# New order tables for all engines and the transfers, up to the first MLP units of a fused adaLN, linear-attention and MLP block

## The chip, the cores and the metric

The kernel runs on one core of a Trainium2 chip. A core has TensorE (PE in the profile, with its weight loads as PEld), VectorE (DVE), ScalarE (ACT), GpSimd (POOL) and a queue of transfers that SyncE issues (SP). The metric is the device time of one execution in microseconds; the median of three runs of the kernel before is 1084.8.

## What is computed

The reference, cut to what matters (S = 2048 tokens, D = 576, F = 4608, H = 32 heads of 18):

```python
mod = (silu(c) @ w_mod).reshape(1, 6, 1, D)
sa, ca, ga, sb, cb, gb = (mod[:, k] for k in range(6))
h = layernorm(x) * (1 + ca) + sa
q, k, v = heads(h @ wqkv)
pq, pk = phi(q), phi(k)             # phi(t) = where(t > 0, t + 1, exp(t)) + 1e-6
kv = einsum("bhsd,bhse->bhde", pk, v);  z = pk.sum(2)
o = einsum("bhqd,bhde->bhqe", pq, kv) / (einsum("bhqd,bhd->bhq", pq, z) + 1e-6)
x = x + ga * (o @ wo)
h = layernorm(x) * (1 + cb) + sb
x = x + gb * (silu(h @ w1) @ w2)
```

All in and out is float32.

## The kernel before

The program is one function without loops at run time: Python loops write out about 19,000 instructions. It has three parts.

*Stage A* (lines 500 to 1336): the mod columns come from w_mod by sums on VectorE (`add_rows`, L516 and L518, into a tile named hT), which TensorE turns into columns (L527) and, for the last chunk, into rows (`mod_rows`, L538, tile psG) and back into columns (L549); `keep_busy` (L567) puts products of ones between, whose results nobody reads. x is transposed (L556, L1250), its layer norm applied (L351 to L365), and K products for the first block of tokens are `k_part` (L573, tile psK, 56 products of 288 columns). Later blocks' K and Q products are L928. phi goes over ACT and DVE, and splits its result in a high and a low half (L958, L960, tile w); TensorE adds xs transposed times these into psG (L1053), block after block, and DVE adds psG to the sums (L1063, tiles sum_107 to sum_111). kv comes from there (L1186), then the product of kv with wo (L1223). The second set of mod rows runs beside all this through GpSimd and a reduction on DVE (L1110, `crow<-raw`).

*Attention out* (200 to 360 us): per block of 512 tokens the transposes L1357, the products L389, the residual, layer norm, and transposes of h into an hT of its own (L374). For pairs of blocks DVE and GpSimd form the sums of a Strassen-like scheme (`sums`, L1684 to L1687: H and S tiles), ACT and DVE split them into two float16 halves (L1631 and L261 among others), and `store_h` (L1508) sends these combinations, named hd, to device memory. Beside this the first slice of the MLP runs as plain products: up L1432, SiLU and split L1434 and L264 to L267 (tile hs), down L1443 in a PSUM tile `big`, and its addition to the token's accumulator on DVE (`down_add`, L1448, tile acc).

*MLP units* (from about 357 us to the end): Strassen-like up products (L1924) and down products (L2008), with VectorE sums (L1946 to L1948 and L2017 to L2021). The combinations hd are fetched back from device memory into three rooms in turn (`fetch`, L1627, tiles hT, xn, first, w), the raw weights of a unit come by `load1` (L1587 and L1589: 512 KB and two of 64 KB) and `load2` (L1596), and the scan of later weights for their scale by L719.

What sets the order: each engine runs its instructions strictly in the order in which they stand in its stream, and SP issues its transfers in the order in which they stand in its own; an instruction whose operand isn't there holds up all that stand behind it. Stage A is first placed by tables named STAGE_A, the units by a list scheduler. Then `arrange(ORDERS, begun)` (L2379) takes the instructions of each engine in the order in which the program traced them and chains them, by dependencies without a wait, in the order of a table of index ranges, ORDERS. Indices that the table doesn't name follow in the traced order:

```python
def arrange(orders, start):
    for engine, text in orders.items():
        traced = [i for i in nc.cur_bb.bb.instructions[start:]
                  if i.engine == getattr(mybir.EngineType, engine) and listed(i)]
        order = [j for part in text.split() for j in span(part)]
        order += sorted(set(range(len(traced))) - set(order))
        for a, b in zip(order, order[1:]):
            follow(traced[b], traced[a])
```

The table names the first 2991 instructions of TensorE, 656 of VectorE, 489 of ScalarE, 262 of GpSimd and 203 of SP. Waits for operands come from the tiles and are set apart from this.

Of the kernel before, what the change touches and what calls it, by code (L numbers as in the profile page):

```python
# [24 lines left out]
def kernel(ctx: ExitStack, tc, A_x, A_wqkv, A_wo, B_x, B_w1, B_w2, c, w_mod, out):  # L25
# [33 lines left out]
    def behind(instructions):  # L59

        with ExitStack() as order:
# [7 lines left out]
            0-43 45-46 52 49-50 44 47-48 53-54 51 65 57-58 61-62 66-72 55-56 59-60 63-64 73-77 82-83 80-81 78-79  # L69
            84-87 90-91 88-89 92-101 116-118 102-103 124 104-105 119-123 125 106-115 126-141 154-167 142-153  # L70
            168-181 246-251 210-213 182-199 214-215 290-293 216-219 294-295 200-209 220-221 256-267 274-277
            222-223 278-289 224-237 302-307 238-245 252-255 308-311 268-273 330-335 296-301 336-357 312-319
            358-359 320-325 360-367 326-329 368-375 378-383 376-377 386-389 384-385 398-403 390-393 404-405
            394-397 412-423 436-451 406-411 424-435 452-477 490-499 478-489 524-527 500-513 520-523 530-539
            514-519 586-587 528-529 588-589 540-545 554-571 576-579 592-597 590-591 598-599 610-621 600-609
            546-551 646-647 580-581 622-627 582-585 552-553 572-575 648-657 670-671 628-641 672-675 682-683
            642-645 684-687 714-721 658-663 722-723 664-665 692-693 666-669 688-689 694-713 724-725 676-679
            726-727 690-691 728-729 680-681 742-745 730-741 746-791 826-831 792-795 862-863 796-797 864-867
            832-833 872-873 798-813 838-839 814-815 840-853 816-821 854-855 822-823 856-859 874-877 860-861
            868-871 878-889 834-837 890-895 824-825 896-917 926-935 918-921 936-939 922-923 940-947 924-925  # L80
            978-983 1000-1003 950-955 966-975 1004-1005 976-977 984-993 948-949 994-999 1006-1019 1022-1023
            1020-1021 956-965 1024-1035 1050-1055 1036-1049 1056-1063 1084-1085 1064-1077 1102-1105 1086-1087
            1106-1113 1078-1079 1114-1117 1088-1091 1118-1123 1130-1131 1080-1081 1132-1135 1124-1129 1136-1137
            1082-1083 1138-1155 1096-1099 1092-1095 1160-1169 1156-1157 1170-1171 1100-1101 1172-1183 1158-1159
            1184-1219 1236-1237 1248-1259 1220-1221 1285-1286 1222-1227 1238-1247 1228-1235 1287-1296 1260-1262
            1297-1300 1263-1284 1301-1325 1352-1356 1326-1349 1357-1364 1385-1388 1365-1370 1389-1390 1350-1351
            1371-1384 1413-1416 1391-1400 1417-1427 1401-1406 1428-1429 1407-1412 1430-1443 1446-1449 1444-1445
            1451-1468 1450 1479-1486 1469-1478 1507-1511 1487-1506 1512-1535 1540-1544 1536-1539 1545-1568
            1573-1574 1569-1572 1575-1592 1601-1604 1593-1594 1605-1621 1595-1596 1634 1638 1597-1600 1622-1633
            1646-1649 1635-1636 1650 1639-1641 1655-1660 1687-1696 1637 1661-1676 1642-1645 1677-1682 1715-1719  # L90
            1697-1700 1651-1654 1701-1704 1683 1705-1706 1720-1723 1684-1686 1707-1714 1724-1751 1762-1767
            1776-1779 1781-1782 1768-1769 1780 1752-1753 1783-1794 1754-1761 1795-1798 1770-1772 1799-1800
            1773-1775 1801-1810 1821-1825 1854 1870-1873 1855-1857 1826-1835 1811-1820 1836-1843 1874 1858
            1875-1877 1844-1853 1859-1860 1883 1915 1884-1886 1861-1863 1916-1918 1878-1881 1887-1888 1882
            1864-1869 1889-1914 1919-1921 1931-1935 1976 1922-1927 1936-1939 1928-1930 1990-1993 1940-1941 1994
            1977-1978 1995-1996 1942-1971 2004-2007 1972-1975 1979-1982 2008-2010 1983-1984 2011-2012 1985-1988
            2013-2018 1989 2019-2036 1997-2003 2037 2049-2061 2082-2083 2098-2101 2062-2069 2086-2088 2070-2077
            2038-2045 2084-2085 2046-2048 2078-2081 2089 2102-2103 2090-2093 2106-2110 2094 2111-2112 2104
            2113-2114 2095-2097 2115-2122 2105 2123-2140 2143 2141-2142 2147 2159-2166 2144-2145 2167-2172 2146
            2173-2178 2187 2179-2186 2188 2199-2202 2189-2190 2203 2191 2204-2210 2213-2214 2148-2149 2215-2216  # L100
            2192-2198 2211-2212 2150-2158 2217 2231-2234 2218-2223 2235-2238 2224-2230 2239-2241 2249 2259-2262
            2245 2255-2258 2246-2248 2242 2263-2264 2243-2244 2265-2269 2295 2250 2296-2299 2251-2253 2270
            2309-2313 2254 2283 2271 2284-2285 2277-2278 2286-2293 2300 2294 2301-2302 2314 2303 2279 2304-2308
            2272-2276 2280-2282 2315-2324 2329 2335-2338 2325 2339-2340 2330-2331 2326-2328 2341 2332-2334
            2347-2356 2342-2346 2359-2360 2357 2361-2369 2358 2370-2377 2391 2378-2382 2392-2398 2383 2399-2404
            2384-2390 2405-2422 2427-2431 2423-2424 2433-2438 2432 2445-2450 2425-2426 2463-2470 2439-2444
            2451-2454 2483-2488 2503-2505 2457-2462 2489-2490 2506-2508 2455-2456 2555-2557 2521-2528 2471-2472
            2477 2473 2478 2474 2567 2479-2480 2475 2481-2482 2541-2542 2476 2543-2544 2568-2572 2545-2546 2491
            2547-2548 2558-2560 2492-2495 2497-2500 2496 2501-2502 2579-2584 2509-2520 2585-2586 2529-2537
            2593-2595 2538-2540 2549-2550 2596-2600 2551-2554 2561-2566 2607-2612 2573-2578 2587-2591 2619-2626  # L110
            2592 2633-2640 2601-2606 2647-2652 2613-2615 2627-2629 2616-2618 2630-2632 2659-2661 2641-2646
            2653-2654 2662-2663 2655-2658 2664-2692 2739-2740 2693-2698 2705-2708 2741-2742 2709-2710 2699-2704
            2733-2735 2719-2720 2743 2711-2718 2721-2732 2736-2738 2744-2762 2783-2794 2775-2782 2815-2820
            2795-2798 2873 2799-2800 2874-2875 2801 2763-2764 2802 2765 2876 2766-2767 2877-2878 2768-2774
            2833-2840 2803-2814 2853-2860 2821 2841 2822 2891 2842-2844 2929 2892-2895 2823-2830 2845-2852
            2930-2936 2879-2881 2909-2912 2831-2832 2882-2887 2913-2915 2888-2890 2916 2861-2867 2896-2898
            2868-2872 2899-2908 2949-2953 2917-2919 2954 2920-2921 2937-2939 2922-2928 2967-2974 2940-2943
            2955-2962 2944-2948 2963-2965 2987-2990 2975-2977 2966 2978-2986
        """,
        "DVE": """  # L120
# [2290 lines left out]
```

## Time and profile before

| | |
|---|---|
| three runs | 1084.69, 1084.8, 1085.23 us |
| span of the profiled execution | 1085.1 us |
| TensorE busy | 1063.3 us, 98% of the span |
| weight loads | 760.6 us, 70% |
| VectorE busy | 893.0 us, 82% |
| ScalarE busy | 707.3 us, 65% |
| GpSimd busy | 737.6 us, 68% |
| device memory | 177 GB/s over the span, read 176.77 MB, written 15.48 MB |
| granted TensorE clock | 0.93 in the first 25 us, 1.00 in each later window |

The profile is of one execution, 0.3 us longer than the median of the runs. A line of the timeline gives the start, the time from there to the end of the last of a run of like instructions, the engine, the line of the kernel, the operation with its tiles, and in brackets the engine's idle time before it and what ended that. A row of the waits gives the waiting line, the releaser, the idle time in total, how often, and the longest. Matmuls overlap, so a matmul's own length is longer than the distance from one start to the next.

### The profile page before, as it was taken

The numbers are of one execution on the slowest core, as the hardware profiler recorded it, in microseconds if no ns is written. First come the engines' busy times: TensorE is split into PE (matmuls) and PEld (weight loads), VectorE is DVE, ScalarE is ACT, GpSimd is POOL, SyncE is SP. The second block draws the span as 40 slices with busy tenths as digits, with TensorE's granted clock in tenths as the row PEclk, the third lists the DMA queues.
The fourth block names the chain that finished last, engine by engine and source line by source line (L and its number), as shares of the span: only waits on it lengthen the run. The fifth ranks groups of instructions, "written<-read, shape, count | busy, mean of one in ns | idle before, by whom it ended". The sixth has DMA issues, their size and how long they took to land.

```text
span 1085.1 us, 19052 instructions
## 1 busy us (share of the span) xinstructions
PE 1063.3 (98%) x7027; PEld 760.6 (70%) x7027; DVE 893.0 (82%) x1438; ACT 707.3 (65%) x1318; POOL 737.6 (68%) x804
## 2 busy tenths in 40 slices
PE   8999999999999899999999999999999999999998
PEld 6999999898885455666666666666666666666665
DVE  7966857788889899988987988987987887898767
ACT  4866553248667777777667667767766776676554
POOL 3467524654725589879888778877778678677563
PEclk9999999999999999999999999999999999999999
DMA  8497954224256877387577577567667657626422
GB/s 294 143 178 202 101 148 119 70 83 127 61 165 195 240 250 254 125 250 230 175 223 213 182 217 222 171 223 203 200 196 234 201 154 252 206 68 201 165 80 109
DMA packets 119341, 193.50 MB, mean 178 GB/s; under 512 B 42892, under 2 KB 77584, under 8 KB 119248
## 3 DMA queue, kind: packets, MB, share of 16 engines
q1 hardware_dynamic: 86276, 190.81, 56.6%
q10 hardware_dynamic: 32972, 1.48, 3.1%
q8 instruction: 55, 0.90, 0.4%
q14 instruction: 38, 0.31, 0.1%
HBM read 176.77 MB, written 15.48 MB: 177 GB/s over the span
## 4 chain that ended last, share of the span: by engine, by line
PE 80%; DVE 9%; DMA 4%; ACT 2%; POOL 2%; issue 1%; SPq 0%; DVEq 0%; POOLq 0%; ACTq 0%
PE up L1924 31%; PE down L2008 30%; PE big L389 5%; PE psK L928 4%; PE psG L1053 4%; PE big L1443 2%; DMA raw<-parts 1%; DMA hT<-hd 1%; PE small L1432 1%; DVE hT L261 1%; PE small L374 1%; DMA raw<-in_w_mod_dram 1%; DVE w L261 1%; PE big L1357 1%; PE psK L1223 1%
## 5 line engine op out<-in xcount | busy, mean ns | idle before, releaser
L1924 PE MATMUL up<-hT,w 128*128 128x512 f16 x1264 | 317.9, 379 | 2.2 <-DMA hT<-hd 2.2
L1924 PEld LDWEIGHTS <-w 128*128 128x128 f16 x1492 | 145.8, 98 | 136.1 <-DMA hT<-hd 2.9
L2017 DVE SCALAR_TENSOR_TENSOR acc<-acc,set,down 128x576 f32<-128x576 f32 x128 | 103.6, 810 | 33.8 <-PE down L2008 32.9
L1942 ACT ACTIVATE f<-f,set 128x512 f32<-128x512 f32 x102 | 73.3, 719 | 63.6 <-DVE f L1948 52.1
L1962 POOL TENSOR_TENSOR s<-f,f 128x256 f32<-128x256 f32 x66 | 54.6, 827 | 77.4 <-ACT f L1943 75.3
L2008 PE MATMUL down<-w,hc 128*128 128x288 f16 x600 | 90.6, 286 | 0.1
L2008 PE MATMUL down<-w,hb 128*128 128x288 f16 x600 | 89.3, 286 | 0.6 <-DVE U L2019 0.5
L2008 PE MATMUL down<-w,hT 128*128 128x288 f16 x480 | 82.8, 286 | 0.4 <-DVE acc L2021 0.4
L1946 DVE TENSOR_TENSOR f<-up,p 128x512 f32<-128x512 f32 x102 | 69.6, 682 | 13.8 <-PE up L1924 9.4
L1943 ACT ACTIVATE f<-f,set 128x512 f32<-128x512 f32 x102 | 73.6, 722 | 3.2
L2008 PEld LDWEIGHTS <-hb 128*128 128x128 f16 x600 | 58.7, 98 | 22.7 <-issue 1.4
L2008 PEld LDWEIGHTS <-hc 128*128 128x128 f16 x600 | 58.7, 98 | 22.0 <-issue 0.4
L1986 POOL TENSOR_TENSOR hc<-s,hc 128x512 f16<-128x512 f32 x50 | 63.9, 1278 | 6.0 <-ACT hc L1982 6.0
L1948 DVE TENSOR_TENSOR f<-up,f 128x512 f32<-128x512 f32 x68 | 46.8, 689 | 25.4 <-PE up L1924 24.3
L2008 PEld LDWEIGHTS <-hT 128*128 128x128 f16 x480 | 46.9, 98 | 26.6 <-issue 0.8
L1966 POOL TENSOR_TENSOR f<-f,s 128x256 f32<-128x256 f32 x66 | 53.4, 809 | 17.3 <-DVE hb L1986 10.2
L1959 POOL TENSOR_TENSOR s<-f 128x256 f32<-128x256 f32 x66 | 57.0, 864 | 9.5 <-ACT f L1939 4.5
L1964 POOL TENSOR_TENSOR s<-s,f 128x256 f32<-128x256 f32 x66 | 56.3, 853 | 3.5
L389 PE MATMUL big<-w,qT 128*128 128x288 f32 x352 | 58.6, 304 | 0.0
L2008 PE MATMUL down<-w,hd 128*128 128x288 f16 x396 | 55.5, 286 | 0.2 <-DVE acc L2017 0.2
L2008 PE MATMUL down<-w,ha 128*128 128x288 f16 x396 | 55.7, 286 | 0.0
L1053 PE MATMUL psG<-w,xs 128*128 128x288 f32 x336 | 52.2, 296 | 1.3 <-DVE sum L1063 1.3
(408 smaller groups left out, 2805.3 us busy)
## 6 DMA issues: line engine op xcount, KB each, us to landing
hT<-hd SPq DMA_DIRECT2D x101, 640.0 KB, 4.6
hT<-hd SPq DMA_DIRECT2D x65, 512.0 KB, 3.7
hT<-in_B_w_dram SPq DMA_DIRECT2D x14, 576.0 KB, 6.4
hT<-in_B_w_dram SPq DMA_DIRECT2D x28, 256.0 KB, 5.8
raw<-in_B_w_dram SPq DMA_DIRECT2D x11, 576.0 KB, 6.2
v<-in_B_w_dram SPq DMA_DIRECT2D x9, 576.0 KB, 4.9
acc<-in_A_x_dram SPq DMA_DIRECT2D x16, 288.0 KB, 4.3
raw<-in_B_w_dram SPq DMA_DIRECT2D x9, 512.0 KB, 5.2
```

The source lines that it names most:

```text
L389: T.matmul(ps, xpart(a), wpart(b), start=n == 0, stop=n == len(XW) - 1)
L1053: T.matmul(ps[:, h, :HALF], l, pk[t][:, u, h * HALF : (h + 1) * HALF], start=t == 0 and m == 0, stop=t == 3 and m == len(left) - 1)
L1924: T.matmul(ps, left, right, start=first and m == 0, stop=m == len(seq) - 1, skip_group_check=True)
L1942: A.activation(f, f, AF.Silu, scale=factor(self.g, "inv"))
L1943: A.activation(f, f, AF.Identity, scale=factor(self.g, "delta"))
L1946: V.tensor_add(f, self.bank[bank[1]], self.p1)
L1959: G.tensor_sub(self.s3, half(i, 0, 0), half(i, 0, 1))
L1962: G.tensor_add(self.s[:, 0:1], half(i, 0, 1), half(i, 1, 1))
L1964: G.tensor_sub(self.s[:, 1:2], self.s[:, 0:1], half(i, 0, 0))
L1986: eng.tensor_sub(t[:, :, 1, :], src, t[:, :, 0, :])
L2008: T.matmul(ps[:, p, :HALF], left[:, u, p * P : (p + 1) * P], right[:, v], start=n in (1, 5, 7, 6) and j == 0, stop=j == len(passes) - 1, s ...
L2017: V.scalar_tensor_tensor(dst, dst, factor(self.g, "ratio"), ps[:, :, :HALF], op0=ALU.mult, op1=ALU.add)
```

## The change

The five tables of ORDERS are replaced by others, found offline. No instruction is altered, added or left out, and each new table names the same indices as the old. STAGE_A and all else are the same. The new tables take 13 lines more, so that every line behind them has a number 13 higher in the changed kernel (L1448 becomes L1461, L1627 becomes L1640).

```diff
     ORDERS = {
         "PE": """
-            0-43 45-46 52 49-50 44 47-48 53-54 51 65 57-58 61-62 66-72 55-56 59-60 63-64 73-77 82-83 80-81 78-79
...
+            0-19 22-23 26 31-35 27-28 38 41-42 20-21 24-25 29-30 36-37 51 39-40 65 52 66-70 43 71-72 45-46 49-50 73-77
...
```

The instructions of the two kernels stand in the same order from about 450 us of the profile before on. Ahead of that most of them move, by a few microseconds of the engine's work. Three places:

TensorE at the head of the program: `psK<-w,hT` are the K products, `psG<-hT,ones` and `psG<-tmod,sc` the mod rows, `psG<-ones` the products that only keep TensorE busy, `psG<-ident` the rows turned into columns. Before:

```order
L527 MATMUL psG_116<-ones,hT 128x1 x2
L567 MATMUL psG_117<-ones 128x128
L527 MATMUL psG_116<-ones,hT 128x1 x2
L567 MATMUL psG_117<-ones 128x128 x2
L573 MATMUL psK<-w,hT 128x288 x3
L538 MATMUL psG_116<-tmod,sc 1x320
L573 MATMUL psK<-w,hT 128x288 x7
L538 MATMUL psG_117<-tmod,sc 1x320
L538 MATMUL psG_117<-hT,ones 1x320
L573 MATMUL psK<-w,hT 128x288 x4
L538 MATMUL psG_116<-hT,ones 1x320
```

and now:

```order
L540 MATMUL psG_116<-ones,hT 128x1 x2
L551 MATMUL psG_117<-tmod,sc 1x320
L540 MATMUL psG_116<-ones,hT 128x1 x2
L551 MATMUL psG_117<-hT,ones 1x320
L551 MATMUL psG_116<-tmod,sc 1x320
L551 MATMUL psG_116<-hT,ones 1x320
L580 MATMUL psG_117<-ones 128x128 x4
L586 MATMUL psK<-w,hT 128x288
L562 MATMUL psG_117<-ident,e 128x1
L562 MATMUL psG_117<-ident,zsum 128x1
L586 MATMUL psK<-w,hT 128x288 x4
```

The first K product has moved behind all four row products, ten of the others with it.

VectorE in stage A, at about 130 to 141 us of the profile before: `w<-a,w` is the low half of phi, `sum<-psG,sum` empties a PSUM bank, `crow<-raw` is the long reduction. Before:

```order
L1020 STREAM_TRANSPOSE acc_94<-xt 128x18x32 x4
L494 SCALAR_TENSOR_TENSOR a<-z,a 128x576
L494 SCALAR_TENSOR_TENSOR a<-e,a 128x576
L960 SCALAR_TENSOR_TENSOR w<-a,w 128x576 x2
L1063 TENSOR_TENSOR sum_107<-psG_116,sum_107 128x576
L1110 TENSOR_REDUCE crow<-raw_122 128x9
L1063 TENSOR_TENSOR sum_108<-psG_117,sum_108 128x576
```

and now:

```order
L1033 STREAM_TRANSPOSE acc_94<-xt 128x18x32 x4
L507 SCALAR_TENSOR_TENSOR a<-z,a 128x576
L507 SCALAR_TENSOR_TENSOR a<-e,a 128x576
L1123 TENSOR_REDUCE crow<-raw_122 128x9
L507 SCALAR_TENSOR_TENSOR a<-z,a 128x576
L973 SCALAR_TENSOR_TENSOR w<-a,w 128x576 x2
L1076 TENSOR_TENSOR sum_107<-psG_116,sum_107 128x576
L374 TENSOR_SCALAR acc_93<-acc_93,col_a 128x512 x2
L1076 TENSOR_TENSOR sum_108<-psG_117,sum_108 128x576
```

The reduction has moved from behind w and the first sum to ahead of both. On TensorE the first product that reads w of the token tile xs_114 has 836 matmuls ahead of it now, and 872 before.

VectorE and SP from the last plain MLP products to the first Strassen-like ones, 338 to 374 us. VectorE: `acc` is the addition of a down product, `H` and `S` are the sums of the combinations. Before:

```order
L267 SCALAR_TENSOR_TENSOR hs<-sl,set_99,hs 128x512
L261 TENSOR_TENSOR hT<-sl,hT 64x512
L1684 TENSOR_TENSOR H<-H,S 128x512
L1685 TENSOR_TENSOR S<-S 128x512
L1448 SCALAR_TENSOR_TENSOR acc_93<-acc_93,set_99,big 128x576
```

and now:

```order
L280 SCALAR_TENSOR_TENSOR hs<-sl,set_99,hs 128x512
L274 TENSOR_TENSOR hT<-S,hT 128x512
L1461 SCALAR_TENSOR_TENSOR acc_93<-acc_93,set_99,big 128x576
L274 TENSOR_TENSOR hT<-S,hT 128x512
L274 TENSOR_TENSOR hT<-sl,hT 64x512
L1697 TENSOR_TENSOR H<-H,S 128x512
L1698 TENSOR_TENSOR S<-S 128x512
```

SP, where `hT<-hd` fetches a combination and `raw` and `hT<-in_B_w` are weights. Before:

```order
L1627 DMA hT<-hd_2140 128x2048
L1589 DMA raw<-in_B_w_dram 64x256
L1587 DMA raw<-in_B_w_dram 128x4x256
L719 DMA hT<-in_B_w_dram 64x4x256 x2
L1627 DMA hT<-hd_2141 128x2560
L1627 DMA hT<-hd_2142 128x2560
L1627 DMA hT<-hd_2133 128x2048
```

and now:

```order
L1640 DMA hT<-hd_2140 128x2048
L1602 DMA raw<-in_B_w_dram 64x256
L1521 DMA hd_2142<-hT 128x512
L1640 DMA hT<-hd_2141 128x2560
L1640 DMA hT<-hd_2142 128x2560
L1602 DMA raw<-in_B_w_dram 64x256
L732 DMA hT<-in_B_w_dram 64x4x256
L1640 DMA hT<-hd_2133 128x2048
L1609 DMA raw<-in_B_w_dram 128x2x576
L1640 DMA hT<-hd_2134 128x2048
L1600 DMA raw<-in_B_w_dram 128x4x256
```

The addition to acc has moved ahead of the sums on VectorE, and on SP the fetches of hd_2141 and hd_2142 ahead of the 512 KB of raw weights and of the weights for the scan; a store of a part of hd_2142 stands right in front of them.

229 lines of the change are left out of this document (121 added, 108 removed).

## The prediction

> **What bounds the kernel now.** I read the page's busy shares first, then the busy time by stretches of the program, then the waits of TensorE, and last the timeline at the few places where TensorE waits longest. The change reaches only up to about 450 us, so the question at each step is how much of TensorE's time ahead of 450 us is not work. The first line of the page, and the windows (span of the window, then busy time of PE, PEld, DVE, ACT, POOL with their instructions, granted clock, DMA share, GB/s):
>
> ```profile
> PE 1063.3 (98%) x7027; PEld 760.6 (70%) x7027; DVE 893.0 (82%) x1438; ACT 707.3 (65%) x1318; POOL 737.6 (68%) x804
> ...
> 0.00:36.00 36.00, 30.96 (x186) 25.60 (x187) 27.59 (x66) 19.91 (x38) 11.49 (x15) 0.95 0.78 255
> 36.00:240.00 204.00, 200.06 (x1478) 196.44 (x1477) 147.34 (x252) 106.88 (x166) 113.63 (x87) 1.00 0.59 131
> 240.00:359.00 119.00, 114.06 (x809) 93.00 (x808) 106.69 (x191) 80.99 (x136) 56.31 (x54) 1.00 0.47 146
> 359.00:450.00 91.00, 87.75 (x507) 49.12 (x506) 82.87 (x132) 70.72 (x145) 76.06 (x93) 1.00 0.69 214
> ...
> 325.00:425.00 100.00, 93.97 (x560) 54.59 (x559) 91.49 (x145) 72.79 (x143) 69.30 (x81) 1.00 0.75 231
> 450.00:475.00 25.00, 25.00 (x170) 16.42 (x169) 22.56 (x36) 17.17 (x35) 19.71 (x25) 1.00 0.68 213
> ```
>
> TensorE is the bound: 98% busy, and full in the window from 450 us on. Ahead of 450 us it is idle for 5.04 us up to 36, 3.94 up to 240, 4.94 up to 359 and 3.25 up to 450 (each window less its first number): 17.2 us. That is the ceiling of any gain from order alone, since the tables change no product. And because TensorE is full right behind 450 us, whatever it gains or loses before goes through to the end one for one.
>
> Where the 17.2 us lie is told by TensorE's waits from 240 to 359 us and then the longest from 359 to 450 us (waiting line, releaser, total, times, longest):
>
> ```profile
> PE big L1443 <- DVE acc L1448: 1.9, 1, 1.9
> PE up L1924 <- DVE acc L1448: 0.8, 1, 0.8
> PE big L1443 <- ACT hs L264: 0.7, 1, 0.7
> PE big L1443 <- DVE qT L261: 0.5, 1, 0.5
> PE big L1443 <- DVE hs L267: 0.5, 1, 0.5
> PE big L1357 <- DVE qT L261: 0.3, 1, 0.3
> PE small L374 <- ACT sl L1434: 0.3, 1, 0.3
> ...
> PE up L1924 <- DMA hT<-hd: 2.2, 1, 2.2
> ```
>
> Two waits of about 2 us stand out, the first row of each part. Both are a matter of who stands in front in a queue, which is what the tables set.
>
> **The change part by part.** Nothing is removed or added; instructions only stand elsewhere. A wait that goes is a gain by its length; an instruction that now stands ahead of its operand makes one.
>
> *The accumulator behind the sums (338 to 342 us).* DVE and, last, TensorE around the 1.9 us:
>
> ```profile
> 338.83 1.65 DVE L1684 TENSOR_TENSOR H<-H,S 128x512 f32<-128x512 f32 x1
> 340.58 1.11 DVE L1685 TENSOR_TENSOR S<-S 128x512 f32<-128x512 f32 x1
> 341.61 0.80 DVE L1448 SCALAR_TENSOR_TENSOR acc<-acc,set,big 128x576 f32<-128x576 f32 x1
> ...
> 342.47 1.88 PE L1443 MATMUL big<-w,hs 128*128 128x288 f16 x14 [1.87 <-DVE acc L1448]
> ```
>
> The addition to acc frees the PSUM bank that the next down product writes. It takes 0.80 us, but two strips of Strassen sums (1.65 and 1.11 us) run in front of it. In the new DVE table the first acc addition stands ahead of both, so it can end 2.8 us earlier than 342.41, before TensorE reaches its product at 340.6. The wait is 1.87 us and should go whole: **-1.9**. What comes late instead is the sums, by the 0.80 us of the addition: they are stored as hd and fetched from there for the MLP units, some 20 us later (the next rows), so there is cover.
>
> *The stored combination behind weight loads (361 to 374 us).* SP's issues, TensorE's wait, and the time to landing of the transfers of this stretch (queue, count, KB each, median us):
>
> ```profile
> 361.43 0.47 SPq L1589 DMA_DIRECT2D raw<-in_B_w_dram  x1
> 361.96 0.58 SPq L1587 DMA_DIRECT2D raw<-in_B_w_dram  x1
> 362.63 1.29 SPq L719 DMA_DIRECT2D hT<-in_B_w_dram  x2
> 366.24 9.74 SPq L1627 DMA_DIRECT2D hT<-hd  x4
> ...
> 374.17 1.47 PE L1924 MATMUL up<-hT,w 128*128 128x512 f16 x6 [2.17 <-DMA hT<-hd]
> ...
> hT<-hd SPq DMA_DIRECT2D x4, 640.0 KB, 7.7
> xn<-hd SPq DMA_DIRECT2D x1, 640.0 KB, 4.0
> ...
> hT<-in_B_w_dram SPq DMA_DIRECT2D x3, 256.0 KB, 7.8
> raw<-in_B_w_dram SPq DMA_DIRECT2D x1, 512.0 KB
> raw<-in_B_w_dram SPq DMA_DIRECT2D x1, 64.0 KB, 4.1
> ...
> hT<-hd SPq DMA_DIRECT2D x101, 640.0 KB, 4.6
> ```
>
> The fetch of hd_2141 is issued at 366.24 and releases TensorE at 374.17, 7.9 us later, while a fetch of the same size in the same stretch, with nothing large ahead of it (xn), took 4.0, and over the whole program the median is 4.6 (the last row, of the page). Ahead of the slow one in the queue are 1,088 KB of weights (64, 512 and two of 256 KB). In the new SP table both fetches (2141 and 2142) stand ahead of the 512 KB and of the two of 256 KB. The issue itself can hardly be earlier, since it waits for the up products to leave its room. So it lands at 366.24 + 4.0 to 4.6 = 370.2 to 370.8, before the 372.0 at which TensorE asks for it: **-2.2**. If the transfers behind it share the engines from the start, 7.9 stays, and the term is nothing. The weights land later by the 1,280 KB now ahead, some 4 us; they are split and used units later.
>
> *The other waits from 240 to 359 us.* They are 0.8 + 0.7 + 0.5 + 0.5 + 0.3 + 0.3 = 3.1. Counting the work ahead of each waiting product and of its releaser in both orders, with the durations of this trace, the releasers of the larger ones (hs, the last acc before L1924) stand 1.3 to 3.6 us nearer to the front than their products do. That speaks for all of it, but such counts hold only while the engine that releases is not itself held up. I take half, **-1.5**, with 0 and -3.1 as bounds.
>
> *The head (0 to 36 us).* TensorE's K products (L573) and what they stand among:
>
> ```profile
> 14.69 0.80 PE L573 MATMUL psK<-w,hT 128*128 128x288 f32 x3 [0.59 <-ACT hT L365]
> 16.05 1.21 PE L573 MATMUL psK<-w,hT 128*128 128x288 f32 x7
> 18.78 0.70 PE L538 MATMUL psG<-hT,ones 128*1 128x320 f32 x2 [0.90 <-DVE hT L518]
> 20.93 1.23 PE L538 MATMUL psG<-hT,ones 128*1 128x320 f32 x2
> 33.77 2.47 PE L928 MATMUL psK<-wq,hT 128*128 128x288 f32 x17
> ...
> 15.89 2.84 DVE L518 SCALAR_TENSOR_TENSOR hT<-hT,sc 128x640 f32<-128x640 f32 x2
> ```
>
> Before, 10 of the 56 K products run while DVE still adds up the mod rows, and the K block is done at 33.8. In the new PE order all four row products (L538) stand ahead of the first K product. They need DVE's last L518, which ends at 15.89 + 2.84 = 18.73, so the first K product starts at about 19.5 instead of 14.7, with TensorE almost idle before. From there on the block is tighter: 56 products at 0.13 us each (the row of 17 on L928: 2.47 / 17 = 0.145, less its tail) are 7.3 us, and the small products among them (L567, L549, L1250) some 5, so 31.8 without any wait. With about 1 us of waits, as much as the block of before had behind 24 us, it is 32.8 against 33.8: **-1.0**. Bounds: -2.6 when the block starts early and waits for nothing; +4.8 when the whole block moves by its later start, 19.5 - 14.7.
>
> [...] The granted clock is 0.95 up to 36 us and 1.00 in each later window. [...]
>
> *New waits.* Nothing in the trace has their length, so I bound them by the places where an order comes closest to its operand. The nearest is stage A from 130 to 142 us:
>
> ```profile
> 132.03 1.62 DVE L960 SCALAR_TENSOR_TENSOR w<-a,w 128x576 fp32r<-128x576 f32 x2 [1.25 <-ACT w L958]
> 138.07 0.76 DVE L1063 TENSOR_TENSOR sum<-psG,sum 128x576 f32<-128x576 f32 x1 [4.42 <-PE psG L1053]
> 138.74 2.33 DVE L1110 TENSOR_REDUCE crow<-raw 128x9 f32<-128x1152 f32 x1
> ...
> 136.28 0.95 PE L1053 MATMUL psG<-w,xs 128*128 128x288 f32 x6
> ```
>
> In before the low half w is ready at 133.65 and its first product starts at 136.28, 2.6 us in hand. In the new orders that product stands 36 products nearer to the front (4.7 us at 0.13), and on DVE the reduction of 2.33 us stands ahead of w: up to 4.7 + 2.3 - 2.6 = 4.4 us of wait, from which comes what DVE's 4.42 idle us take up. Bounds for all new waits are 0 and 9 (two or three such places, as below). I take **+2.0**, nearer to nothing, since DVE is busy only 147.34 of 204.00 us from 36 to 240 and can catch up.
>
> **Sum.** -1.9 - 2.2 - 1.5 - 1.0 + 2.0 = -4.6. The profiled span is 1085.1 us and the median of the runs shown 1084.8, 0.3 less; taken off the median, 1084.8 - 4.6 = **1080.2**.
>
> **The rivals.**
> *Slower: stage A starves.* The 4.4 us at w come whole, and the sums L1063, which stand behind the same reduction and w, hold the next PSUM bank for another 2 to 3 us, then once more at the last block of stage A: three waits of 3 us. Gains kept: -6.6; new waits +9.0; sum +2.4, 1087.2. For it: TensorE waits 1.3 us for those sums in this stage already, twice. Against it: DVE is idle over a quarter of this stretch. It decides against the change once the new waits are over 6.6 + 2.2 us.
> *No change: VectorE takes it back.* From 325 to 425 us DVE is busy 91.49 of 100 us. If TensorE comes 4.1 us earlier, DVE must do the same work with half of its 8.5 us of idle time, and its order is bound to PSUM banks that come free one by one. The two large waits then come back as waits for L2017 and L2021 behind 375 us: -1.5 - 1.0 + 2.0 = -0.5, 1084.3. Against it: DVE's 22.56 of 25 us in the window from 450, where TensorE waits for nothing.
> *No change: the head loses.* +4.8 in place of -1.0, the other terms kept: +1.2, 1086.0. For it: TensorE starts K 4.8 us later, and what it did in that time still has to be done. Against it: the small products that kept it from K behind 19 us are then done. The clock: its loss up to 36 us, 0.05 x 36 = 1.8 us, is paid once more on the K block: -4.6 + 1.8 = -2.8, 1082.0.
> *More.* All waits of 240 to 374 us go and none is new: -1.9 - 2.2 - 3.1 - 1.0 = -8.2, 1076.6.
> That the change doesn't do what it says is no rival: the listed order has the moves.
>
> **How the numbers follow.** A measurement of this kernel can tell some 0.2%, 2.2 us, from no change: under 1082.6 is faster, over 1087.0 slower. Forecast 0.45, the clock's case 0.05, more 0.10: faster 0.60. VectorE 0.16 and the head 0.07: same 0.23. Stage A 0.17: slower. The range goes from all terms at their best with no new wait, -1.9 - 2.2 - 3.1 - 2.6 = -9.8, 1075.0, to stage A's 1087.2; the likeliest case alone holds 1077 to 1082.6.
>
> **What would show each step.** Right: no wait of L1443 for acc over 0.5 us near 340, none of L1924 for hd near 370, hd_2141 landing within 5 us of its issue, L928 beginning at or before 33.8, TensorE full from 450 us on but with everything 4 to 5 us earlier. Wrong: waits of psG for sum or w of over 2 us between 128 and 150 us, waits for L2017 or L2021 of over 1 us between 375 and 450, a granted clock under 0.95 up to 36 us, or a stretch before 240 us that ends later than now. The prediction falls if the time is over 1082.6, and its reason falls if the time is under it but both 2-us waits are still there.

## The result, and the profile after

The changed kernel took 1090.57 us in the median of 4 runs (1090.06 to 1093.48), the kernel before 1084.74 beside it (1083.59 to 1085.23). The ratio is 1.0064, with an interval of 1.0048 to 1.0080: slower by about 6 us, where 1080.2 was forecast and 1087.2 was the upper end.

The profiled execution of the changed kernel has a span of 1088.6 us and took 1090.37, so a time is its span and some 1.75 us. By that the profile of before (span 1085.1) is of an execution of about 1086.9, and not of a typical one: 73 further runs of before, in three groups, lie between 1081.5 and 1087.3, with medians of 1083.98, 1083.96 and 1084.09.

First the busy times of the page and the same four windows as before (span, then busy PE, PEld, DVE, ACT, POOL, granted clock, DMA share, GB/s), of the changed kernel:

```profile
PE 1066.5 (98%) x7027; PEld 763.9 (70%) x7027; DVE 872.1 (80%) x1438; ACT 707.4 (65%) x1318; POOL 732.8 (67%) x804
...
0.00:36.00 36.00, 30.74 (x198) 27.19 (x199) 27.32 (x74) 23.15 (x46) 11.12 (x15) 0.95 0.84 270
36.00:240.00 204.00, 198.45 (x1439) 193.90 (x1438) 130.68 (x233) 105.78 (x162) 105.73 (x84) 0.98 0.61 134
240.00:359.00 119.00, 115.36 (x810) 94.56 (x809) 99.30 (x190) 77.50 (x126) 59.78 (x55) 0.99 0.38 120
359.00:450.00 91.00, 87.67 (x511) 49.47 (x509) 82.63 (x136) 68.08 (x139) 72.73 (x89) 1.00 0.76 235
```

TensorE's idle time is now 5.3, 5.6, 3.6 and 3.3 us, 17.8 in all against 17.2: the order gained nothing on balance. And the same 7027 products kept it busy for 1066.5 us instead of 1063.3, with a granted clock of 0.98 and 0.99 where before had 1.00. The 0.6 us of waits and the 3.2 us of slower products are the 3.5 us between the two spans, to a few tenths.

Then TensorE's waits of the changed kernel from 240 to 359 us and, last, from 359 to 450 us (waiting line, releaser, total, times, longest):

```profile
PE small L1445 <- ACT hT L1653: 1.1, 1, 1.1
PE small L1445 <- DVE hT L274: 1.0, 2, 0.7
PE small L387 <- DVE xn L366: 0.7, 1, 0.7
PE big L1370 <- DVE acc L1461: 0.4, 1, 0.4
PE big L1456 <- DVE acc L1461: 0.2, 1, 0.2
...
PE up L1937 <- DMA hT<-hd: 2.9, 2, 2.6
```

The waits that the prediction named are gone: none for acc near 340 us beyond the 0.2 of the fifth row, none for hd near 370 (the 2.6 us of the last row stand at 432). Others have come. Where, is told by comparing when TensorE has done the same amount of work in the two traces. By that lag (plus is later) the changed kernel loses 16.3 us in four short stretches and gains 12.5 elsewhere:

| stretch, us of before | lag gained or lost | lag at its end |
|---|---|---|
| 0 to 90 | -2.4 | -2.4 |
| 90 to 100 | +3.6 | +1.2 |
| 100 to 210 | -2.4 | -1.2 |
| 210 to 230 | +4.8 | +3.7 |
| 230 to 320 | -0.9 | +2.8 |
| 320 to 340 | +4.6 | +7.4 |
| 340 to 420 | -6.0 | +1.4 |
| 420 to 430 | +3.2 | +4.6 |
| 430 to the end | -0.8 | +3.8 |

The 6.0 us from 340 to 420 hold what was forecast for the accumulator and the fetch. The four losses are these.

*The accumulator's load, 210 to 230 us.* The changed kernel's issues of SP, then DVE and TensorE that wait for the last of them (start, length, and in brackets the idle time before):

```profile
209.73 0.34 SPq L815 DMA_DIRECT2D acc<-in_A_x_dram  x1
210.24 1.32 SPq L732 DMA_DIRECT2D w<-in_B_w_dram  x2
211.66 0.56 SPq L1389 DMA_DIRECT2D raw<-in_B_w_dram  x1
212.26 0.50 SPq L800 DMA_DIRECT2D acc<-in_A_x_dram  x1
...
219.31 0.76 DVE L1384 TENSOR_TENSOR acc<-big,acc 128x576 f32<-128x576 f32 x1 [6.54 <-DMA acc<-in_A_x_dram]
...
220.12 1.07 PE L402 MATMUL big<-w,qT 128*128 128x288 f32 x6 [3.05 <-DVE acc L1384]
```

and the same load in the kernel before:

```profile
198.80 4.33 SPq L787 DMA_DIRECT2D acc<-in_A_x_dram  x2
```

The new SP table sets this load of x behind three loads of weights, whose own turn doesn't come before 210 us. It goes out 13.5 us later, behind their bytes, and lands 7.0 us after its issue; DVE stands 6.54 us for it, and TensorE 3.05 for DVE.

*The reduction, 90 to 100 us.* DVE and TensorE of the changed kernel:

```profile
83.06 2.40 DVE L1123 TENSOR_REDUCE crow<-raw 128x9 f32<-128x1152 f32 x1 [2.70 <-DMA raw<-parts]
85.39 2.72 DVE L1033 STREAM_TRANSPOSE acc<-xt 128x576 f32<-128x576 f32 x4
...
89.62 0.53 PE L1066 MATMUL psG<-w,xs 128*128 128x288 f32 x2 [0.70 <-ACT w L971]
90.97 0.53 PE L1066 MATMUL psG<-w,xs 128*128 128x288 f32 x2 [0.83 <-DVE w L973]
```

DVE's reduction stands in front of its transposes and of the steps that make w, and waits 2.70 us for its own transfer. All behind it is late, and TensorE waits 0.70 us for w's high half and 0.83 for its low one.

*The cast, 320 to 340 us.* ACT and TensorE of the changed kernel:

```profile
329.03 1.62 ACT L364 ACTIVATE xn<-acc,mv 128x576 f32<-128x576 f32 x2 [4.15 <-PE small L387]
330.56 0.60 ACT L1653 CAST hT<-H 128x512 f16<-128x512 f32 x1
...
331.21 0.59 PE L1445 MATMUL small<-hT,w 128*128 128x512 f16 x2 [1.11 <-ACT hT L1653]
```

ACT's cast hT stands behind a layer norm that waits 4.15 us for TensorE, and TensorE waits 1.11 us for the cast. Of the rows of waits above, 0.38 of the second, the 0.71 of the third (DVE's layer norm behind the residual addition) and the 0.17 of the fifth lie in this stretch too: 2.4 us in all. The other 0.66 of the second row stands at 270 us.

*The store, 420 to 430 us.* SP and TensorE of the changed kernel:

```profile
425.08 0.42 SPq L746 DMA_DIRECT2D limits<-raw  x1
427.17 0.32 SPq L1640 DMA_DIRECT2D hT<-hd  x1
...
434.55 0.38 PE L1937 MATMUL up<-hT,w 128*128 128x512 f16 x1 [2.55 <-DMA hT<-hd]
```

The fetch of hd_2142 now stands behind a store of limits, is issued at 427.17 and releases TensorE 7.4 us later. The wait before it, 0.32 us for a fetch, lies in this stretch too.

The losses are larger than the waits in them: 3.6 for 1.5 (0.70 + 0.83), 4.8 for 3.05, 4.6 for 2.4, 3.2 for 2.9 (2.55 + 0.32). The trace records TensorE's granted clock, and behind three of the four waits it falls to one half. Windows of the changed kernel, two by two, the one with the wait and the next:

```profile
88.00:91.40 3.40, 1.88 (x12) 1.41 (x12) 2.56 (x4) 2.61 (x4) 1.41 (x1) 1.00 0.75 216
91.48:94.89 3.41, 3.41 (x17) 3.41 (x16) 1.39 (x2) 0.97 (x2) 3.16 (x2) 0.50 0.76 201
217.80:221.10 3.30, 0.98 (x7) 0.98 (x8) 1.79 (x3) 2.77 (x4) 0.00 (x0) 1.00 0.41 102
221.19:224.60 3.41, 3.41 (x17) 3.41 (x16) 2.38 (x6) 0.00 (x0) 2.26 (x2) 0.50 0.44 127
330.40:333.80 3.40, 1.50 (x8) 0.76 (x8) 2.89 (x8) 2.38 (x5) 1.99 (x3) 1.00 0.97 325
333.83:337.24 3.41, 3.41 (x13) 1.71 (x14) 1.66 (x2) 1.46 (x2) 3.41 (x4) 0.50 0.38 100
```

What such a window costs is read from the distance between products. The first two rows lie in the second window of half clock, the others behind it:

```profile
221.37 1.65 PE L402 MATMUL big<-wq,hT 128*128 128x288 f32 x6
222.81 1.17 PE L402 MATMUL big<-w,qT 128*128 128x288 f32 x4
...
225.47 0.70 PE L402 MATMUL big<-w,qT 128*128 128x288 f32 x4
226.00 0.42 PE L402 MATMUL big<-v,qT 128*128 128x288 f32 x2
```

Six products take 222.81 - 221.37 = 1.44 us, 0.24 each; behind the window four take 0.53, 0.13 each. So a window full of these float32 products costs 3.41 x (1 - 0.13 / 0.24) = 1.5 us; float16 ones of 512 columns stand 0.43 us apart in the window from 333.83 (three from 333.93 to 335.23) and 0.22 behind it (three from 338.43 to 339.08), which makes 1.7. Then 1.5 + 1.5 = 3.0 stand for 3.6 measured, 3.05 + 1.5 = 4.6 for 4.8, 2.4 + 1.7 = 4.1 for 4.6, and without a window 2.9 for 3.2. The four places are thereby accounted for, to 0.6 us each. Each of the three windows of half clock is 3.41 us long in the trace, and in the 3.3 to 3.4 us ahead of each TensorE worked for 0.98 to 1.88 us.

### The profile page after: what moved, and what is told of

It reads as the page before. It is cut to its first block, busy times and chain, and to the rows that moved or that the text cites. A ratio compares the mean times of both kernels' runs of the same rounds, so it can differ in the third digit from the quotient of the medians.

```text
span 1088.6 us, 19038 instructions
## 1 busy us (share of the span) xinstructions
PE 1066.5 (98%) x7027; PEld 763.9 (70%) x7027; DVE 872.1 (80%) x1438; ACT 707.4 (65%) x1318; POOL 732.8 (67%) x804
## 4 chain that ended last, share of the span: by engine, by line
PE 77%; DVE 5%; DMA 4%; ACT 1%; issue 1%; SPq 0%; POOL 0%; DVEq 0%; ACTq 0%; POOLq 0%
PE up L1937 32%; PE down L2021 30%; PE big L402 5%; PE psK L941 2%; PE psG L1066 2%; PE small L1445 1%; DMA hT<-hd 1%; PE big L1456 1%; DVE hT L274 1%; DMA acc<-in_A_x_dram 1%; DMA acc<-turned 1%; PE big L1370 1%; PE small L387 1%; PE down L2055 1%; PE up L2055 1%
## 5 line engine op out<-in xcount | busy, mean ns | idle before, releaser
L1937 PE MATMUL up<-hT,w 128*128 128x512 f16 x1264 | 322.0, 379 | 2.9 <-DMA hT<-hd 2.9
L2021 PE MATMUL down<-w,hc 128*128 128x288 f16 x600 | 91.4, 286 | 0.0
L2021 PE MATMUL down<-w,hb 128*128 128x288 f16 x600 | 91.3, 286 | 0.1
L2021 PE MATMUL down<-w,hT 128*128 128x288 f16 x480 | 82.8, 286 | 0.4 <-DVE acc L2034 0.4
L2021 PEld LDWEIGHTS <-hb 128*128 128x128 f16 x600 | 58.7, 98 | 25.9 <-issue 3.2
L2021 PEld LDWEIGHTS <-hc 128*128 128x128 f16 x600 | 58.6, 98 | 22.6 <-POOL hc L1999 0.2
L402 PE MATMUL big<-w,qT 128*128 128x288 f32 x352 | 62.7, 311 | 3.0 <-DVE acc L1384 3.0
L2021 PEld LDWEIGHTS <-hT 128*128 128x128 f16 x480 | 46.9, 98 | 26.6 <-issue 0.8
L1066 PE MATMUL psG<-w,xs 128*128 128x288 f32 x336 | 55.6, 296 | 1.5 <-DVE w L973 0.8
L2021 PE MATMUL down<-w,ha 128*128 128x288 f16 x396 | 56.5, 286 | 0.1
L2021 PE MATMUL down<-w,hd 128*128 128x288 f16 x396 | 56.3, 286 | 0.0
```

Of the source, the lines that this page charges most:

```text
L402: T.matmul(ps, xpart(a), wpart(b), start=n == 0, stop=n == len(XW) - 1)
L1066: T.matmul(ps[:, h, :HALF], l, pk[t][:, u, h * HALF : (h + 1) * HALF], start=t == 0 and m == 0, stop=t == 3 and m == len(left) - 1)
L1937: T.matmul(ps, left, right, start=first and m == 0, stop=m == len(seq) - 1, skip_group_check=True)
L2021: T.matmul(ps[:, p, :HALF], left[:, u, p * P : (p + 1) * P], right[:, v], start=n in (1, 5, 7, 6) and j == 0, stop=j == len(passes) - 1, s ...
```

## The experiments

Edits that move instructions are shown as rows of the order. A kernel's lines have other numbers where its table takes fewer lines; the tiles name the row. Runs of one group share the runs of before.

**The two moves of the forecast alone**, on the kernel before; DVE's, then SP's:

```diff
 TENSOR_TENSOR hT<-sl,hT 64x512
+SCALAR_TENSOR_TENSOR acc_93<-acc_93,set_99,big 128x576
 TENSOR_TENSOR H<-H,S 128x512
 TENSOR_TENSOR S<-S 128x512
-SCALAR_TENSOR_TENSOR acc_93<-acc_93,set_99,big 128x576
...
 DMA raw<-in_B_w_dram 64x256
-DMA raw<-in_B_w_dram 128x4x256
-DMA hT<-in_B_w_dram 64x4x256 x2
 DMA hT<-hd_2141 128x2560
 DMA hT<-hd_2142 128x2560
+DMA raw<-in_B_w_dram 128x4x256
+DMA hT<-in_B_w_dram 64x4x256 x2
```

> The kernel before with only two of the moves of the change: VectorE's addition to acc ahead of the two strips of sums near 339 us, and SP's fetches of hd_2141 and hd_2142 ahead of the 512 KB of weights near 362 us. Theory (both predicted gains are real and the loss lies elsewhere): both 2-us waits of TensorE go, -1.9 -2.2 = -4.1, 1080.6. Rival (VectorE and the transfers take it back behind): the two waits come back within 80 us as others, within 1 us of 1084.7.

1090.24 us (6 runs), ratio 1.0053 (1.0032 to 1.0075): slower by 6 us, where the forecast's steps promised 4.1 less. Both were then run apart.

**The fetches alone.** The second half of the edit above.

> The kernel before with only the move on SP: the fetches of hd_2141 and hd_2142 ahead of the 512 KB of raw weights and the two loads for the scan. My prediction's term: -2.2, 1081.8. Theory from the run with both moves (the weights now stand ahead of the fetch of hd_2133, which lands 9 us after its issue, and ScalarE waits for the scan's loads): the wait at 372 goes, waits of 3.0 and 2.0 us at 382 and 386 and a half-clock window or two come, -2.2 +5.0 +2 = +4.8, 1088.8.

1090.2 us (6), 1.0060 (1.0047 to 1.0073): as much by itself as both moves together. The wait at 372 us is gone; behind it stand these, in SP's, ACT's and TensorE's rows of this kernel:

```profile
369.09 0.43 SPq L1575 DMA_DIRECT2D raw<-in_B_w_dram  x1
369.62 1.83 SPq L707 DMA_DIRECT2D hT<-in_B_w_dram  x2
372.54 2.04 SPq L1615 DMA_DIRECT2D hT<-hd  x2
...
379.95 1.06 ACT L708 ACTIVATE hT<-hT 128x1024 f32<-128x1024 f32 x1 [5.24 <-DMA hT<-in_B_w_dram]
...
381.95 1.53 PE L1912 MATMUL up<-hT,w 128*128 128x512 f16 x3 [2.08 <-ACT w L252]
384.88 2.72 PE L1912 MATMUL up<-S,w 128*128 128x512 f16 x6 [1.40 <-DVE f L1934]
```

The weights that stood ahead of one fetch now stand ahead of the next two. The scan of the weights on ACT, which the prediction passed over with "units later", waits 5.24 us for its load and holds up the split of w behind it. 2.08 + 1.40 us of waits follow, and half clock from 382.54 to 389.4. The lag against before jumps by 6.3 us between 380 and 390, which is 3.5 of waits and 2.8 of the 3.4 that two half-clock windows can cost. This run is not the changed kernel's order of that place: there the 512 KB and the second load for the scan stand behind the next two fetches as well, TensorE has no such waits, and the stretch gains 6.0.

**The accumulator alone.** The first half of the edit.

> The kernel before with only the move on VectorE: the addition to acc ahead of the two strips of sums near 339 us. My prediction's term: -1.9, 1082.1. Theory from the run with both moves (VectorE has the same work in front of a later addition to acc): the wait at 340 goes, one of 1.7 us comes at 350, +0.5 with a half-clock window behind it now and then, 1084.5.

1087.68 us (6), 1.0038 (1.0027 to 1.0050). The wait near 340 us is gone, and TensorE waits at 348 (DVE's and TensorE's rows of this kernel):

```profile
342.33 1.68 DVE L1674 TENSOR_TENSOR S<-S,H 128x512 f32<-128x512 f32 x1
...
347.05 1.52 DVE L1436 SCALAR_TENSOR_TENSOR acc<-acc,set,big 128x576 f32<-128x576 f32 x2
...
347.90 0.28 PE L1431 MATMUL big<-w,hs 128*128 128x288 f16 x1 [1.50 <-DVE acc L1436]
```

One acc addition earlier, the next ones as late as ever: the 1.87 us come back 8 us further on as 1.50 and 0.44, both for VectorE's acc, and with them comes a half-clock window at 349.6 that the 1.87 had not brought. From 340 to 360 us of before TensorE is idle for 3.2 us in both traces, and the lag rises by 1.67: that is the price of the window alone. The profile shows no more than this of the 3.6 us; the runs have 3.2 such windows in the mean, before's beside them 1.0.

**The late load alone**, on the kernel before, SP:

```diff
-DMA acc_91<-in_A_x_dram 128x576 x2
+DMA acc_91<-in_A_x_dram 128x576
 DMA raw<-in_B_w_dram 64x256
 DMA w<-in_B_w_dram 64x4x256
 DMA acc_91<-in_A_x_dram 128x576
 DMA w<-in_B_w_dram 64x4x256
+DMA raw<-in_B_w_dram 128x4x256
+DMA acc_91<-in_A_x_dram 128x576
 DMA acc_91<-in_A_x_dram 128x576
...
-DMA raw<-in_B_w_dram 128x4x256
```

The 512 KB of raw weights come two places forward, to stand ahead of the load as in the new order.

> The kernel before with only SP's first load of x into acc_91 (issued at 198.8 us before) moved behind two weight loads for the scan and one of raw weights, as in the new order. Theory (a wait of TensorE costs itself and, when it leaves TensorE idle for most of a 3.4-us window, one more window at half clock): a wait of some 3 us for the addition to acc near 217 us and a half-clock window of 3.41 us behind it, +3.0 +1.7 = +4.7, 1089.4. Rival (the half-clock windows of the new order come by chance and not from its waits): a wait of 3 us and no such window, +3.0, 1087.7. Second rival (the kernel of before has slack behind there): within 1 us of 1084.7.

1086.33 us (10), 1.0024 (1.0004 to 1.0043). In its profile the load goes out at 209.70 instead of 198.80, and TensorE waits 1.1 us for acc at 216, a third of what was expected; no half clock followed there, the granted clock of that execution is 1.000. The lag against before rises by 1.3 us between 210 and 220.

**The load put back** in the changed kernel, ahead of the other loads of x:

```diff
-DMA acc_91<-in_A_x_dram 128x576
+DMA acc_91<-in_A_x_dram 128x576 x2
 DMA acc_91<-in_A_x_dram 128x576
 DMA w<-in_B_w_dram 64x4x256 x2
 DMA raw<-in_B_w_dram 128x4x256
-DMA acc_91<-in_A_x_dram 128x576
```

> The changed kernel with only that load put back ahead of the other loads of x. Theory: the 3.3-us gap of TensorE at 217 us goes with the half-clock window behind it, -3.0 -1.7 = -4.7 against the changed kernel, 1085.9. Rival (windows by chance): -3.0, 1087.6 with as many half-clock windows as before.

1088.05 us (10), 1.0033 (1.0018 to 1.0049) in place of the changed kernel's 1.0064: some 3 of the 6 us come back by one entry of SP's table. That is the size that the rival named, and the runs have 2.8 half-clock windows in the mean, as many as the changed kernel's 3.0. In the profile both the wait and the window at 217 us are gone; two windows stand at 16.5 us and one at 432.9.

**Three moves undone** in the changed kernel: that load, and

```diff
-TENSOR_REDUCE crow<-raw_122 128x9
 STREAM_TRANSPOSE acc_94<-xt 128x18x32 x4
 SCALAR_TENSOR_TENSOR a<-e,a 128x576
+TENSOR_REDUCE crow<-raw_122 128x9
...
-DMA limits_4340<-raw 128x2
 DMA hT<-hd_2142 128x2560
+DMA limits_4340<-raw 128x2
```

> The changed kernel with three moves undone: that load; on VectorE the long reduction, which waits for its transfer at 83 us, put behind the transposes and one addition of stage A; on SP the store of the limits put behind the fetch of hd_2142 near 427 us. Theory: the waits at 89 (2.0), 217 (3.0) and 432 us (2.6) and the two half-clock windows behind the first two go: -7.6 -3.4 = -11.0, 1079.6. Rival (each wait that goes uncovers another behind it, since the order is tight all through): half of that, 1085.

1085.13 us (10), 1.0002 (0.9989 to 1.0015): level with before, near the rival's 1085 and far from 1079.6. The three moves together carry the loss. In its profile the lag against the changed kernel falls by 4.5 us between 205 and 240 us, at the load. It falls by 2.5 between 85 and 100, at the reduction, and 2.4 of that come back up to 205 as other waits (the longest 1.56 us, for a sum of stage A). At the store the wait falls from 2.55 to 1.59. So only the load's part shows by itself, and the forecast of 11 us failed at least in part because a wait that goes uncovers another.

**The changed kernel again**, beside the next three.

> The changed kernel itself, beside the others on the same chip, for its own spread and its count of half-clock windows. Theory (its loss is new waits and the half-clock windows that they bring): 1090.5, with a mean granted clock of about 0.995, three windows of 3.41 us, against one or two in the kernel before. Rival (the windows fall by chance in both alike): the same mean clock as before.

1092.02 us (6), 1.0076 (1.0061 to 1.0091). Its profile has the same four places, so they belong to the order and not to one execution; half clock follows behind each of the four (two of these windows start at 223.03 and 438.07 us), and the granted clock of the execution is 0.989:

```profile
PE up L1937 <- DMA hT<-hd: 4.1, 2, 2.9
PE big L402 <- DVE acc L1384: 3.5, 1, 3.5
PE psG L1066 <- ACT w L971: 1.8, 1, 1.8
...
PE small L1445 <- ACT hT L1653: 1.1, 1, 1.1
```

**The head alone**: the new order for what starts ahead of 60 us in the changed kernel's profile, and the old one behind.

```diff
-order = new
+head = [i for i in new if start[i] < 60]
+order = head + [i for i in old if i not in head]
```

> The kernel before with the new order of all engines for what the changed kernel starts before 60 us, and the old order behind. My prediction's term for the head: -1.0, 1083. Theory from the trace of the changed kernel, which stands 2.4 us ahead at 60 us: -2.4, 1081.6. Rival (the one profiled execution of before had a bad head, and the two heads are alike): within 0.7 us of before.

1085.64 us (12), 1.0023 (1.0009 to 1.0037). Its profile stands at -0.2 us at 60, but the seam itself makes a wait of 2.2 us at 77 and half clock behind it, so the 1.7 us are not the head's price. That is better read from all profiled executions, by the start of the first Q product: 32.80 us over nine with the old head (31.17 to 34.71), 33.31 over eight with the new one (31.41 to 34.52). The head loses half a microsecond or nothing.

**More undone**: the three, and four further steps set back (a 512 KB load behind the fetches, one sum ahead of the statistics, the residual ahead of the layer norm, and, as below, ACT's cast).

```diff
+CAST hT<-H 128x512
 ACTIVATE xn<-acc_94,mv 128x576 x2
-CAST hT<-H 128x512
```

> The changed kernel with the three moves undone as before, and three more places mended: the 512 KB of raw weights ahead of the fetches near 417 us put behind them, VectorE's addition to sum_109 ahead of the layer norm's statistics near 105 us, and near 326 us the residual addition with its statistics ahead of the transposed chunk, and ScalarE's cast of hT ahead of the layer norm. Theory (each named wait is worth its length): 1.7 + 1.8 + 2.4 us less than with three undone, 1085.1 - 5.9 = 1079.2. Rival (others take their place): half, 1082.

1084.31 us (12, 1079.87 to 1087.79), 1.0001 (0.9987 to 1.0015): no further gain, where 1079.2, or 1082 by the rival, was expected. The profile, of the fastest of the 12 runs, does show that the steps do something: from 320 to 340 us, where the cast stands, it loses 1.7 us against before, the kernel with three moves undone 3.5.

**The wait filled.** In the changed kernel 24 products with the identity stand in front of the product that waits at 217 us, so that TensorE isn't idle while it waits. The lines of TensorE's chain and of the product:

```diff
+    if call == 2 and n == 7:
+        fill.append(at.ins)
+        for _ in range(24):
+            fill.append(T.matmul(outs[0][0][:, :P], ident, plus1[:, 0:1].to_broadcast([P, P]), start=False, stop=False).ins)
...
+    at = [i is fill[0] for i in chain].index(True) + 1
+    chain[at:at] = fill[1:]
```

> The changed kernel with 24 products of the identity by zeros, added to a tile in progress, put in front of the product that waits near 217 us; they add nothing to the result and take some 2.6 of the 3.3 us of the wait. Theory (idle time within a 3.4-us window brings the next window to half clock): the wait stays, no half-clock window behind it, 1.7 us less than the changed kernel when it has one there, some 1.2 on average. Rival (the windows don't come from idle time): as the changed kernel, 1090.5.

1092.64 us (5), 1.0082 (1.0069 to 1.0095), against 1.0076 of the unfilled kernel. The 24 products are 48 matmuls in the trace. DVE's and TensorE's rows of this kernel, then two windows:

```profile
221.13 0.76 DVE L1396 TENSOR_TENSOR acc<-big,acc 128x576 f32<-128x576 f32 x1 [6.55 <-DMA acc<-in_A_x_dram]
...
218.75 5.52 PE L414 MATMUL big<-plus,ident 128*128 128x128 f32 x48
224.02 1.32 PE L410 MATMUL big<-w,qT 128*128 128x288 f32 x8
...
215.50:220.50 5.00, 5.00 (x43) 5.00 (x42) 0.00 (x0) 1.42 (x3) 1.41 (x3) 1.00 1.06 282
220.50:224.00 3.50, 3.50 (x34) 3.50 (x33) 2.62 (x5) 2.30 (x4) 0.71 (x1) 1.00 0.18 50
```

With TensorE busy through the wait the clock stays at 1.00, where the changed kernel fell to half in both of its profiles. But the fill is longer than the wait. DVE's addition ends at 221.13 + 0.76 = 221.89; in the changed kernel the product starts within 0.1 us of that end, here at 224.02, 2.1 us later, behind the rest of the 48. From 216 to 225 us this kernel's products fall 0.5 us further behind those of the changed kernel's profile, which is 2.1 of fill too much less 1.5 of half clock that didn't come. So the medians could show no gain, and the run speaks for the clock by its trace alone.

**Mixed orders**: the old one for what starts ahead of 205 us in the profile of before, and the order with more undone behind; then the same with 320 us.

```diff
-order = old
+first = [i for i in old if start[i] < 205]
+order = first + [i for i in more_undone if i not in first]
```

> All engines in the old order for what the kernel before starts ahead of 205 us, and behind it the changed order with its moves mended as in the run with more undone. Theory (the new order is better only in the first MLP units, from 340 us on, once its new waits are mended, and its head brings a half-clock window that the old one mostly doesn't have): the 3.8 us that the mended kernel gains behind 205 us, 1080.2. Rival (the two orders are alike but for the new waits): 1084, as before.

> The same with the cut at 320 us. Theory: 3.4 us from the stretch behind 320, 1080.6. Rival: 1084, as before, or slower by a wait at the cut.

1083.14 us (12), 1.0001 (0.9986 to 1.0016), and 1084.85 (12), 1.0006 (0.9993 to 1.0019). Their profiled executions took 1081.51 and 1080.94, the runs reach up to 1088.2: neither beats before, where 1080.2 and 1080.6 were expected.

**Three run again**: before, more undone, and the mixed order of 205 us, each once.

> The kernel before, another profiled execution. Theory (its first profile, with a span of 1085.1, lies 2 to 3 us above its median): a span near 1082.4, the same waits at 342 and 374 us within 1 us, and a head that is up to 2.5 us shorter. Rival: a span of 1085 again.

> The changed kernel with six moves undone, another profiled execution. Theory (its spread comes from half-clock windows and from transfers that land late in some executions): a span of 1082 to 1084 against 1078.2 before, with one or two more windows and some wait for a transfer of 1 to 3 us that the first profile hadn't. Rival (all places cost the same each time): 1078 again.

> The kernel with the old order up to 205 us and the mended new one behind, another profiled execution. Theory: a span of 1079 to 1085, differing from its first profile (1079.7) at few places, which are half-clock windows or waits for transfers. Rival: the same everywhere.

1085.36, 1083.41 and 1082.78 us. The profiles of one kernel differ in waits for transfers. Before's second profile has, from 335 to 380 us:

```profile
PE big L1443 <- DVE acc L1448: 1.9, 1, 1.9
PE up L1924 <- DMA hT<-hd: 1.2, 1, 1.2
```

and the mixed order's second profile, near 405 us, a wait that its first one had not:

```profile
PE up L1923 <- DMA hT<-hd: 2.6, 2, 2.2
```

The wait for acc, between engines, is the same to a tenth; the one for hd, for a transfer, is not.

## Why the prediction was wrong, point by point

**The step that failed is the term "New waits": "I take +2.0, nearer to nothing, since DVE is busy only 147.34 of 204.00 us from 36 to 240 and can catch up".** It measured some 10: 1.5 + 3.05 + 2.4 + 2.9. The mean of a stretch said nothing here. In the wait at 217 us DVE had time in plenty, and stood 6.54 us for a load that SP's table had moved. The prediction looked for late operands on one engine at a time and at one place, stage A from 130 to 142 us, and didn't follow SP's queue behind an entry whose turn comes late. The load put back gave 3 us, the three moves undone the whole loss: that new waits carry it is shown, and for the load by itself. How the rest divides among the reduction, the cast and the store is not.

**The clock.** It was priced at the head alone, as a rival with 0.05: the clock's loss up to 36 us, 1.8, paid once more. The changed kernel's profile doesn't show that term, its clock up to 36 us is 0.95 as before's, with one half-clock window in each (at 12.97 and 20.83 us). The loss lies behind the waits: 1.5 to 1.7 us at each of three, some 5 of the 16.3 us lost. From the granted clock of every run the number of such windows comes out as 3.0 for the changed kernel (3.4 when run again) and 1.0 to 1.8 for before.

**The accumulator, -1.9.** The wait went, as said. Alone the move costs 3.6 us: the rival that VectorE takes it back had this mechanism ("two large waits then come back"), but named L2017 and L2021 behind 375 us, where it was the next acc at 348, and it comes back with a half-clock window. In the changed kernel, where the table moves other work too, the stretch from 340 to 420 us gains 6.0.

**The stored combination, -2.2.** The wait went too, and the price was wrong twice. The 2.2 us belong to one execution: four other profiles with before's order of SP there have 1.2, 0.8, 0.3 and nothing. And of the weights moved behind the fetches it was said that they "land later ... some 4 us; they are split and used units later"; alone that move costs 6 us, by the scan's load and the fetches behind it. In the changed kernel those loads stand further back still, and this cost doesn't show.

**The other waits, -1.5.** Outside the stretch of the cast they were 3.1 and are 1.1 (0.66 and 0.41), a gain of 2.0, within the bounds. The sum had no term for the waits of stage A that go: from 36 to 90 and from 100 to 210 us the new order gains 3.2 us.

**The head, -1.0.** It is +0.5 or nothing over the profiled executions, within the bounds. Its first Q row of the changed kernel begins at 32.23, 1.5 earlier than before's 33.77, as forecast; the sample of executions shows that these two single rows prove nothing.

**The baseline.** "The profiled span is 1085.1 us and the median 1084.8, 0.3 less" set a span beside a time. With the 1.75 us between them the profile was of an execution 2 us above the median, and the forecast took a gain from a wait for a transfer that other executions have at 0 to 1.2 us.

**The rivals.** "Stage A starves" had the right side and about the right sum of new waits (9); its place was wrong, since 130 to 142 us lost nothing (the lag is +0.2 at 120 us and 0.0 at 150).

**What stays open.** With the three moves undone the gains of 340 to 420 us should remain. The six profiles of mended kernels have spans of 1078.2 to 1084.1 us, where before's median of 1084.0 stands for 1082.3; but their medians are level with before. Their runs have 1.6 to 2.4 half-clock windows in the mean, as many as before's or more, and fetches that land at other times in each execution; which of these eats the gain was not settled. The clock's share is measured in traces alone, by the distance of the products and by stretches of equal idle time; no median shows it, and the page's busy time of TensorE grew by 3.2 us where three more windows would make 5.

## What to carry to other kernels

A wait that goes when an instruction is moved ahead is not a gain of its length: ask which instruction of the same queue now stands where the moved one stood, and price that first, above all on the queue of transfers, where the load of x, behind three loads of weights, went out 13.5 us later and landed 7.0 us after its issue. Add to a wait the half-clock window that it can bring, here 1.5 to 1.7 us. Check each load that a new order sets later against the time at which its reader starts, not against its engine's mean. And take the length of a wait for a transfer from several executions (the one for hd was 2.2, 1.2, 0.8, 0.3 us and nothing), the profile's own time set beside the median.

## What the runs showed of the hardware

- Half clock, a granted clock of 0.50, stands in the traces in windows of 3.41 us. Before's profile has one ahead of 450 us, at 20.83; the changed kernel's has four, at 12.97, 91.48, 221.19 and 333.83. With the fetches alone half clock lasted from 382.54 to 389.4, two windows in a row. The four starts of the changed kernel's profile are 78.51, 129.71 and 112.64 us apart, 23, 38 and 33 times 3.413; before's one start lies 7.85 us behind the first of them, 2.3 times 3.413.
- What TensorE waited in a stretch of 3.41 us, in steps of that length from these starts, and what came behind it: in the changed kernel's profile 2.35 us (from 217.77), 1.89 (from 330.41) and 1.52 (from 88.07) were followed by half clock, 1.73 (from 432.81) was not. Before's wait of 1.87 us at 342 falls into two such stretches, 1.08 and 0.79, and brought none; of its 2.17 us at 374, 1.77 fell into one, and brought none either.
- Part of the spread of one kernel goes with these windows: of the 73 runs of before, the 27 without any have a mean of 1083.0 us, those with about one (by a granted clock of 0.998 or 0.999) 1083.7, with two (0.996 or 0.997) 1084.7, with three (0.995) 1085.5, some 0.8 us each. That is half of the 1.5 to 1.7 us of a window in full work; before's profile has its one window at 20.83 us, in the head, where TensorE is idle for 5.04 of 36 us.
